# Sums of weight blocks for the last two groups: made on GpSimd alone, their stores asked for later, and one raw quarter stored as it is rounded

## The chip, the core and the metric

The kernel runs on one core of a Trainium2 chip. The metric is the device time of one execution in microseconds (us), as the median of several runs. All of it is in fp32.

## What is computed

Attention in chunks of 64 tokens on 8 batches, 8 heads, 576 tokens and 64 channels, then a mixing block. Cut to what matters:

```python
out = softmax(q_c @ k_c.T / 8) @ v_c                 # chunk by chunk
x = out.transpose(0, 2, 1, 3).reshape(8, 576, 512)
u = x + real(fft2(x))                                # over tokens and channels
un = (u - mean) / sqrt(var + 1e-6)
return u + maximum(un @ w_ch1, 0) @ w_ch2            # 512 -> 2048 -> 512
```

The two weight products are most of the work. `w_ch1` is 512 x 2048, `w_ch2` 2048 x 512; both arrive in 64 bit and are rounded to fp32 on the chip.

## The kernel before, in words

**Groups and steps.** The 4608 tokens are nine groups of 512 (numbers 0 to 8), each of four tiles of 128 rows. A group goes through an *up* product (to 2048 features, `h1`) and a *down* product (back to 512). The generator `mlp(g)` yields after each small part of that; the loop at L1489 counts these yields as *steps* `t`. After each step it hands out a share of the other work: attention and Fourier transform of the next batch, rounding of weight pieces (`round_next`), sums of weight blocks, and loads and stores. No scheduler moves anything: every engine runs its instructions in the order in which this loop writes them down, and so do the queues of transfers. Nearly all transfers are in SyncE's queue, called SP here; some output stores are in ACT's. In the built program each transfer of these two queues waits for the one eight before it.

**Fewer products.** Group 0 multiplies plainly, group 1 plainly in its up product. The other up products, and the down products of groups 1 to 6, split the matrices in halves and use 7 block products in place of 8 (`up_halves`, `down_halves`). In `up_halves` four *pairs* of feature blocks are made one after the other, each in seven *turns* of eight matmul instructions, in the order `UP`. Of a pair, ACT copies a first result (L1272), VectorE adds the others out of PSUM (L1273, L1275, L1277, L1283, L1286), and ACT applies the relu (L1281, L1284, L1287). After each turn SP fetches a slab of summed weights for ten turns later (`fetch(1)`, L1140). In the last turns of pair 2 of groups 7 and 8, GpSimd makes six sums of activation blocks (`EARLY`, L1168).

**26 products in the last two groups.** The down products of groups 7 and 8 (`down_few`, from `FEW = NG - 2`) split finer: 26 products (`PRODUCTS`), of which each reads one block of `w_ch2` or a sum of such blocks. Eighteen sums, the names that begin with s, are used by products (`STORED`). `MADE` lists the 23 operations, intermediate ones too:

```python
MADE = (
    "u=b41-b31", "s3=b31-b41", "s15=u-b42", "s7=u-b11", "s8=b12+b22", "s0=u-s8", "t=b32-b42", "s19=u+t",
    "v=b32-b31", "s10=b11-b12", "s23=v-s10", "s21=s10-b32", "s24=s10-b22", "w=b22-b21", "s22=w-s10",
    "s4=b42-b41", "s25=w+s4", "s1=b21-s4", "s17=b21+b41", "h=b12+b32", "s12=h-s17", "s6=b42-h", "s18=-h",
)
```

`make_rest` does this in two halves, since there is little room: for each it loads the eight raw blocks (L1109), each 128 x 512, makes the sums (L1121, the negation at L1117), and stores the eighteen that are used (L1127) to DRAM (`s3`). It has fourteen places of 128 x 512, kept in the list `spare`: a place is given back when its block is last used, and an operation that takes it again must wait until the store out of it has landed. In before, a store is written into SP's queue when the next used sum has been written down (`behind` holds one), and the work goes to GpSimd for every third operation and to VectorE for the others. `make_rest` is advanced by one or two of its yields after each step from step 203 on, that is in the down product of group 6 and the up product of group 7. At step 225, in the last pair of group 7's up product, what is left of it is written down and the first six slabs of group 7's down product are fetched (`fetch(3)`, L1143).

**Raw quarters.** The blocks that the products read unsummed are stored to DRAM too: three quarters of `w_ch2` by `keep2_whole` (L1079), as the pieces are rounded in group 0, and the last by `keep2_last` (L1083), four stores of 256 KB in steps 32 to 35, at the start of group 1. Rounding of a piece ends with L386 on VectorE; L346 loads the next one. In group 1 SP also carries the loads of k (L250), which VectorE transposes (L416) before a head product (L448) can start.

**Outputs.** When a tile's down product is summed, `store` asks for it: L1027 on SP for one half of the tiles, L1036 on SP and ACT for the other. In group 6 the sums before them are L1335 and L1338 on VectorE. In the same product GpSimd makes L1330 and L1331 and VectorE makes the operands of the next group (L994, L1005, L1015 to L1018).

Of the kernel before, what the change touches and what calls it, by code (L numbers as in the profile page):

```python
# [11 lines left out]
ALU = mybir.AluOpType  # L12
# [4 lines left out]
def kernel(  # L17
# [32 lines left out]
    nc = tc.nc  # L50
# [10 lines left out]
    KF = DFF // 128  # L61
# [41 lines left out]
    NO, HF = 7, KF // 2  # L103
# [989 lines left out]
    def make_rest():  # L1093

        z, spare = Z3 // 2, []
        for i in range(4):
            spare.append(xall[:, 2 * G:2 * G + 4, :].rearrange("p a f -> p (a f)")[:, i * z:(i + 1) * z])
        for tag, n in (("q", 2), ("k", 2), ("zf", 2), ("two", 1), ("qT", 1), ("kT", 1), ("pT", 1)):  # L1100
            t = one_p.tile([128, n * z], FP32, tag=tag, name="part")
            spare += [t[:, i * z:(i + 1) * z] for i in range(n)]
        last = {x: i for i, text in enumerate(MADE) for x in text.replace("=", "-").replace("+", "-").split("-")}
        for half in range(2):
            part = slice(half * z, (half + 1) * z)
            where, behind = {}, []
            for name in ("b31", "b41", "b42", "b11", "b12", "b22", "b32", "b21"):
                where[name] = spare.pop(0)
                nc.sync.dma_start(out=where[name], in_=block_of(name)[:, part])  # L1109
                if name in ("b41", "b11", "b22"):  # L1110
                    yield
            for i, text in enumerate(MADE):
                name = text.split("=")[0]
                to = spare.pop(0)
                if "=-" in text:
                    used = [text.split("-")[1]]
                    nc.vector.tensor_scalar(to, where[used[0]], -1.0, None, ALU.mult)  # L1117
                else:
                    name, *used, op = parsed(text)
                    in0, in1 = (where[x] for x in used)  # L1120
                    (nc.gpsimd if i % 3 == 1 else nc.vector).tensor_tensor(out=to, in0=in0, in1=in1, op=op)  # L1121
                where[name] = to
                if name in STORED:
                    behind.append(name)
                while behind and (len(behind) > 1 or i == len(MADE) - 1):
                    old = behind.pop(0)
                    nc.sync.dma_start(out=block_of(old)[:, part], in_=where[old])  # L1127
                spare += [where[x] for x in (*used, name) if last[x] == i]
                if i % 2:
                    yield  # L1130

    FEW = NG - 2
# [281 lines left out]
    with tc.manual_schedule():  # L1414
        nc.vector.memset(warm, 0.0)
        make_identity(nc, ident)
        nc.vector.memset(eps, 1e-6)
        for r in range(4):
            nc.vector.memset(sign[32 * r:32 * r + 32], 2.0 * (r % 2) - 1.0)
        nc.vector.memset(top[:, 0:1], float((896 + 255) << 20))  # L1420
        nc.vector.memset(top[:, 1:2], float(255 << 23))
        nc.scalar.preload_act_table_set("natural_log_exp_and_others")
        first_rest = three_p.tile([128, XW], FP32, tag="y", name="first_rest")
        for t in more_v + v_ring:
            nc.vector.memset(t[:, :, :, D:DV], 1.0)
        for n in range(first[1]):
            load(n)
            if n < 3:
                load_v(n)
        load_v(3)  # L1430
        load_v(4)
        load_tables()
        load_weight(0)
        load_dim_tables()
        for i in range(1, len(spaces)):
            load_weight(i)
        n_w = 2
        idle = [ps_f.tile([128, 512], FP32, tag="ff", name="idle")]
        early_xp = [ps_f.tile([128, 512], FP32, tag="ff", name="early_xp") for _ in range(2)], None

        def keep_warm(times):

            for _ in range(times):
                nc.tensor.matmul(out=idle[0][:, 0:NQ], lhsT=warm[:, 0:128], rhs=warm[:, 0:NQ], start=True, stop=True)

        put_off, first_ups = [], []

        def round_next(later=None):
            nonlocal n_w
            if n_w <= len(pieces):  # L1450
                round_weight(n_w, later)
                n_w += 1

        keep_warm(8)
        attention_early()
        turn_dim_row()
        for step, _ in enumerate(fourier_early()):
            if step == 0:
                turn_dim_tables()
        round_next()  # L1460
        PAUSE = 3

        def side(b):
            yield from attention(b)
            for _ in range(PAUSE if b == 1 else PAUSE - 1):
                yield
            yield from fourier(b)

        sides = [list_ for list_ in (side(b) for b in range(1, B))]
        sizes = []  # L1470
        for b in range(1, B):
            n_tiles = first[b + 1] - first[b]
            sizes.append((4 * n_tiles + 1 if b == 1 else 3 * n_tiles + 1) + PAUSE + 2 + (b == 1) + NM + b % 2)
        done, cur = 0, 0
        begin = [0]
        for g in range(NG):
            begin.append(begin[-1] + (KF if g < first_of[1] else 2 * HF) + (KF if g < first_of[2] else 2 * NO if g < FEW else NR2 // 2))
        ready_at = [begin[g] + (2 * KF - 7 if g < first_of[2] else 2 * HF + 4) for g in range(NG)]
        conv2 = iter([step for i in range(HF // 2) for step in [keep2(i ^ 1)]])
        conv1 = iter([step for i in range(4) for step in [keep1(i)]])  # L1480

        def chain(gens):
            for gen in gens:
                yield from gen

        n_whole, late, rest_ = 0, [], None
        conv2, conv1 = chain(conv2), chain(conv1)
        t = 0
        for g in range(NG):  # L1489
            for _ in mlp(g):  # L1490
                t += 1
                heavy = False
                for do in late:
                    do()
                late = []
                if t == 8:
                    nc.scalar.copy(tk, early_tk[:, :, :, 0:NE])
                if cur < len(sides):
                    t0 = 3 if cur == 0 else ready_at[cur - 1]
                    t1 = ready_at[cur]  # L1500
                    due = min(sizes[cur], (t - t0) * sizes[cur] // (t1 - t0))
                    while done < due:
                        heavy = next(sides[cur], None) or heavy
                        done += 1
                    if t >= t1:
                        for _ in sides[cur]:
                            pass
                        cur, done = cur + 1, 0
                if not heavy:
                    round_next(late if t < KF and t % 4 == 3 else None)  # L1510
                    if t <= 2 or t < KF and t % 4 == 0 or t >= KF + 3:
                        round_next()

                while n_whole < HF // 2 and n_w > KF + HF + 2 * n_whole + 2:
                    keep2_whole(n_whole)
                    n_whole += 1
                if n_w > len(pieces):
                    for _ in range(3):
                        next(conv2, None)
                if t == begin[1] - 1:  # L1520
                    for _ in conv2:
                        pass
                if begin[1] <= t < begin[1] + HF // 2:
                    keep2_last(t - begin[1])
                if t > ready_at[FEW - 1]:
                    rest_ = rest_ or make_rest()
                    for _ in range(1 + t % 2):
                        next(rest_, None)
                if t == begin[FEW] + 2 * HF - 3:
                    for _ in rest_:  # L1530
                        pass
                    for _ in range(NS3):
                        fetch(3)
                if begin[1] <= t < begin[1] + KF // 2:
                    for _ in range(3):
                        next(conv1, None)
                if t == begin[1] + KF // 2:
                    for _ in range(NS2):
                        fetch(2)
                if t == begin[1] + KF:  # L1540
                    for _ in range(NS1):
                        fetch(1)
# [49 lines left out]
```

## Time and profile before

| what | value |
|---|---|
| median of 4 runs | 1097.84 us (1094.62 to 1098.67) |
| the profiled execution | 1097.19 us, span 1095.4 us |
| busy share of TensorE, VectorE, ACT, GpSimd | 97%, 55%, 28%, 35% |
| mean granted TensorE clock | 0.99 |
| transfers | 219.53 MB, mean 200 GB/s |
| group 6 down (827.0 to 881.5 us) | 54.5 us, TensorE busy 53.31 |
| group 7 up (881.5 to 949.7 us) | 68.2 us, TensorE busy 56.57 |
| group 8 up (996.4 to 1044.7 us) | 48.3 us, TensorE busy 48.30 |

A row of a window gives its bounds, its length, the busy time of TensorE, of its weight load, of VectorE, ACT and GpSimd (in brackets the instructions), the granted clock, the share of the transfer engines and GB/s. A row of the timeline gives start, duration, engine, line, operation, tiles and shapes, and in square brackets how long the engine was idle before it and on whom. A row of waits gives who waited for whom: us in total, times, and the longest. A piece of the chain gives its start, its length and what it is; a transfer's length there is from its issue to its landing. PE is TensorE, DVE is VectorE, POOL is GpSimd, SPq is SyncE's queue. PE's busy time includes its modelled pipeline, so a slow clock shows as longer matmuls.

### The profile page before, as it was taken

The page shows a single profiled execution, that of the slowest core. Times are in us where ns is not written, and L with a number is a line of the kernel's source. Part 1 is how long each engine was busy: PE and PEld are TensorE (multiplying, and loading weights), DVE is VectorE, ACT ScalarE, POOL GpSimd, SP SyncE. Part 2 cuts the span into 40 slices and gives each one's busy share as a digit, 9 for nine tenths or more (in the row PEclk, how much of TensorE's full clock was granted, in tenths as well). Part 3 has the DMA queues.
Part 4 walks back from the last instruction along what each step waited for, and adds up shares of the span by engine and source line. Part 5 has one row for each costly group of instructions (what it writes and reads, how often), then busy time and mean ns, then how long its engine had stood idle before and what let it go on. Part 6 is the DMA issues. An engine that isn't in the chain of part 4 may idle for free.

```text
span 1095.4 us, 19948 instructions
## 1 busy us (share of the span) xinstructions
PE 1059.3 (97%) x7386; PEld 839.2 (77%) x7386; DVE 603.7 (55%) x1305; ACT 310.7 (28%) x728; POOL 387.9 (35%) x509
## 2 busy tenths in 40 slices
PE   8999989999999999999999999999999987999997
PEld 6645444446888888888888888888888866888886
DVE  4798975233567455654565556645655636334331
ACT  4687653212113411322033203330223001201200
POOL 4311017463515140345033401632243414470281
PEclk9999999999999999999999999999999988999999
DMA  8677566598467645873677357935643668887366
GB/s 175 212 208 210 130 183 210 179 313 273 150 190 225 162 165 163 243 212 127 190 208 220 123 160 238 246 114 176 231 135 129 218 208 294 313 303 247 110 220 202
DMA packets 162829, 219.53 MB, mean 200 GB/s; under 512 B 69644, under 2 KB 107532, under 8 KB 157358
## 3 DMA queue, kind: packets, MB, share of 16 engines
q1 hardware_dynamic: 159084, 214.86, 63.5%
q10 hardware_dynamic: 3330, 2.76, 1.0%
q8 instruction: 59, 0.97, 0.4%
q0 software_dynamic: 320, 0.66, 0.3%
q14 instruction: 36, 0.29, 0.1%
HBM read 183.61 MB, written 34.60 MB: 199 GB/s over the span
## 4 chain that ended last, share of the span: by engine, by line
PE 74%; DMA 7%; DVE 6%; POOL 3%; ACT 3%; SPq 3%; issue 3%; ACTq 0%; DVEq 0%; POOLq 0%
PE pa L1267 17%; PE pb L1318 14%; PE pb L1267 12%; PE pa L1318 11%; PE dn L1382 8%; PE up L1200 2%; PE pt L397 2%; DMA s<-part 2%; PE up L1180 2%; PE mix L838 2%; SPq L263 1%; PE z L719 1%; PE xp L498 1%; DMA xall<-in_moe_w_ch_dram 1%; PE sc L448 1%
## 5 line engine op out<-in xcount | busy, mean ns | idle before, releaser
L1267 PE MATMUL pa<-unT,wa 128*128 128x256 f32 x672 | 163.8, 387 | 11.0 <-DVE wa L1275 4.9
L1267 PEld LDWEIGHTS pa<-unT,wa 128*128 128x128 f32 x672 | 127.8, 193 | 31.0 <-DVE wa L1275 6.1
L1267 PE MATMUL pb<-wa 128*128 128x256 f32 x448 | 107.7, 383 | 1.6 <-DVE h L1286 1.6
L1267 PEld LDWEIGHTS pb<-wa 128*128 128x128 f32 x448 | 85.1, 192 | 13.9 <-DVE h L1286 2.0
L1318 PE MATMUL pa<-wb,h 128*128 128x256 f32 x384 | 87.2, 380 | 0.0
L1318 PE MATMUL pb<-wb,h 128*128 128x256 f32 x384 | 86.4, 379 | 0.0
L1318 PEld LDWEIGHTS pa<-wb,h 128*128 128x128 f32 x384 | 71.8, 190 | 9.7
L1318 PEld LDWEIGHTS pb<-wb,h 128*128 128x128 f32 x384 | 72.0, 190 | 9.4
L1154 POOL TENSOR_TENSOR h<-h 128x256 f32<-128x256 f32 x48 | 40.8, 858 | 94.3 <-DVE wb L1152 91.1
L555 POOL COPY xall<-xall 1x512 f32<-1x512 f32 x28 | 17.9, 639 | 147.9 <-DVE xall L515 120.4
L1382 PE MATMUL dn<-wb,h 128*128 128x256 f32 x304 | 67.6, 379 | 0.0
L1382 PEld LDWEIGHTS dn<-wb,h 128*128 128x128 f32 x304 | 57.4, 190 | 7.6
L1273 DVE TENSOR_TENSOR wa<-pb,wa 128x256 f32<-128x256 f32 x56 | 23.7, 424 | 63.9 <-ACT wa L1272 63.9
L1221 PE MATMUL dn<-wb,h 128*128 128x512 f32 x128 | 58.7, 607 | 0.0
L1200 PE MATMUL up<-unT,wa 128*128 128x512 f32 x128 | 58.5, 610 | 0.0
L1168 POOL TENSOR_TENSOR h<-h 128x512 f32<-128x512 f32 x36 | 45.5, 1279 | 33.5 <-ACT h L1287 30.2
L1272 ACT COPY wa<-pa 128x256 f32<-128x256 f32 x56 | 20.9, 373 | 125.4 <-PE pa L1267 94.7
L1267 PE MATMUL pa<-wa 128*128 128x256 f32 x224 | 55.7, 393 | 0.1
L1267 PE MATMUL pb<-unT,wa 128*128 128x256 f32 x224 | 53.2, 380 | 0.0
L1281 ACT ACTIVATE h<-pa 128x256 f32<-128x256 f32 x56 | 21.6, 385 | 106.3 <-PE pa L1267 105.6
L1180 PE MATMUL up<-unT,wa 128*128 128x512 f32 x108 | 49.4, 598 | 0.0
L1267 PEld LDWEIGHTS pa<-wa 128*128 128x128 f32 x224 | 42.9, 195 | 7.3 <-ACT wa L1272 0.8
(290 smaller groups left out, 1993.5 us busy)
## 6 DMA issues: line engine op xcount, KB each, us to landing
wa<-s SPq DMA_DIRECT2D x196, 256.0 KB
wb<-s SPq DMA_DIRECT2D x42, 1024.0 KB
wb<-s SPq DMA_DIRECT2D x52, 512.0 KB
xall<-in_moe_w_ch_dram SPq DMA_DIRECT2D x22, 512.0 KB
q<-in_q_dram SPq DMA_DIRECT2D x96, 112.0 KB
k<-in_k_dram SPq DMA_DIRECT2D x96, 112.0 KB
v<-in_v_dram SPq DMA_DIRECT2D x124, 64.0 KB
s<-part SPq DMA_DIRECT2D x27, 256.0 KB
```

The lines of the kernel that those rows point to most:

```text
L397: nc.tensor.transpose(pt[:, j, :], src(j), ident)
L838: nc.tensor.matmul(out=mix[:, cols], lhsT=zt[:, T], rhs=tab, start=(T == 0), stop=(T == 3), skip_group_check=True,)
L1154: nc.gpsimd.tensor_tensor(out=h1[:, m, hi], in0=h1[:, m, lo], in1=h1[:, m, hi], op=ALU.subtract)
L1168: nc.gpsimd.tensor_tensor(out=out_, in0=a, in1=b, op=op)
L1180: nc.tensor.matmul(out=up, lhsT=w1[:, kk, m * 128:(m + 1) * 128], rhs=unT[:, kk], start=(kk == 0), stop=(kk == KD - 1), skip_group_check=True,
L1200: nc.tensor.matmul(out=up, lhsT=w1[:, kk, m * 128:(m + 1) * 128], rhs=unT[:, kk], start=(kk == 0), stop=(kk == KD - 1),)
L1221: nc.tensor.matmul(out=dn, lhsT=h1[:, m, s * 128:(s + 1) * 128], rhs=w2[:, m, :], start=(m == 0), stop=(m == KF - 1),)
L1267: nc.tensor.matmul(out=dst, lhsT=w[:, kk, r], rhs=rhs[o][:, kk], start=(o in (0, 1) and kk == 0), stop=(kk == 1), skip_group_check=True,)
L1273: nc.vector.tensor_tensor(out=b, in0=pbs[r][:, 0], in1=a, op=ALU.add)
L1281: nc.scalar.activation(out=h1[:, m, lo], in_=dst, func=ACTF.Relu)
L1318: nc.tensor.matmul(out=dst, lhsT=lhs[:, m], rhs=w[:, m], start=(o in (0, 2) and m == 0), stop=(m == HF - 1), skip_group_check=True,)
L1382: nc.tensor.matmul(out=dst, lhsT=lhs[:, m], rhs=w[:, m], start=(fresh and not half and m == 0), stop=(m == 3), skip_group_check=True,)
```

## The change

```diff
@@ make_rest
             for name in ("b31", "b41", "b42", "b11", "b12", "b22", "b32", "b21"):
                 where[name] = spare.pop(0)
                 nc.sync.dma_start(out=where[name], in_=block_of(name)[:, part])
-                if name in ("b41", "b11", "b22"):
+                if half and name in ("b41", "b11", "b22"):
                     yield
+            yield
             for i, text in enumerate(MADE):
                 name = text.split("=")[0]
                 to = spare.pop(0)
                 if "=-" in text:
                     used = [text.split("-")[1]]
-                    nc.vector.tensor_scalar(to, where[used[0]], -1.0, None, ALU.mult)
+                    nc.scalar.mul(to, where[used[0]], -1.0)
                 else:
                     name, *used, op = parsed(text)
                     in0, in1 = (where[x] for x in used)
-                    (nc.gpsimd if i % 3 == 1 else nc.vector).tensor_tensor(out=to, in0=in0, in1=in1, op=op)
+                    nc.gpsimd.tensor_tensor(out=to, in0=in0, in1=in1, op=op)
                 where[name] = to
                 if name in STORED:
                     behind.append(name)
-                while behind and (len(behind) > 1 or i == len(MADE) - 1):
+                done_with = [x for x in (*used, name) if last[x] == i]
+                while behind and (len(behind) > 3 or i == len(MADE) - 1):
                     old = behind.pop(0)
                     nc.sync.dma_start(out=block_of(old)[:, part], in_=where[old])
-                spare += [where[x] for x in (*used, name) if last[x] == i]
+                    if last[old] <= i and old not in done_with:
+                        done_with.append(old)
+                spare += [where[x] for x in done_with if x not in behind]
                 if i % 2:
                     yield
@@ the loop over steps
-                if begin[1] <= t < begin[1] + HF // 2:
-                    keep2_last(t - begin[1])
-                if t > ready_at[FEW - 1]:
-                    rest_ = rest_ or make_rest()
+                while n_last < HF // 2 and n_w > KF + 2 * n_last + 2:
+                    keep2_last(n_last)
+                    n_last += 1
+                if t == ready_at[FEW - 1]:
+                    rest_ = make_rest()
+                    next(rest_)
+                if t > ready_at[FEW - 1] + 4:
                     for _ in range(1 + t % 2):
                         next(rest_, None)
```

- All 44 two-operand sums of `make_rest` go to GpSimd (before: 14, and 30 on VectorE); the two negations go from VectorE to ACT.
- The eight loads of the first half are written down together at step 202 instead of over the first steps from 203; the sums follow from step 207 on instead of right after the loads. The loads of the second half still come in parts, at steps 214 to 216; its sums run to step 224.
- A store is written down when three further used sums have been (`behind` holds three), and a place is not given back before its store has been asked for.
- The four stores of `keep2_last` are written down as soon as the two pieces that they read are rounded, in group 0, among SP's weight loads, instead of in steps 32 to 35.
- TensorE's instructions and their order are the same.

More of the change, by code (lines that the diff above doesn't have):

```diff
@@ L1484, in chain @@
                 yield from gen
-        n_whole, late, rest_ = 0, [], None
+        n_whole, n_last, late, rest_ = 0, 0, [], None
         conv2, conv1 = chain(conv2), chain(conv1)
```

## The prediction

> **What bounds the kernel now.** I read the page's engine shares first, then busy time by windows around the two stages that the diff touches, then TensorE's waits there, the timeline and the chain of waits.
>
> ```profile
> PE 1059.3 (97%) x7386; PEld 839.2 (77%) x7386; DVE 603.7 (55%) x1305; ACT 310.7 (28%) x728; POOL 387.9 (35%) x509
> ...
> 881.50:949.70 68.20, 56.57 (x227) 46.64 (x226) 32.26 (x60) 13.64 (x31) 20.21 (x15) 0.90 0.79 262
> ...
> 996.40:1044.70 48.30, 48.30 (x225) 42.53 (x224) 16.98 (x40) 13.93 (x31) 8.01 (x7) 1.00 0.40 132
> ```
>
> TensorE sets the time, so only its gaps and its slow clock can be won. The two windows are the up products of group 7 and of group 8: the same matmuls take 68.2 us and 48.3 us, so group 7 loses 19.9 us (11.6 idle, the rest at a granted clock of 0.90). Its waits say on whom:
>
> ```profile
> PE pa L1267 <- DVE wa L1275: 3.8, 2, 2.0
> PE pa L1267 <- DVE h L1283: 3.3, 1, 3.3
> PE pa L1267 <- DVE wb L1338: 2.9, 1, 2.9
> PE pb L1267 <- DVE h L1286: 1.6, 1, 1.6
> ```
>
> All four are VectorE evictions standing behind a weight sum (L1121) that waits for a transfer:
>
> ```profile
> 883.64 0.69 DVE L1121 TENSOR_TENSOR part<-part,xall 128x512 f32<-128x512 f32 x1 [4.73 <-DMA s<-part]
> ...
> 889.44 3.78 PE L1267 MATMUL pa<-wa 128*128 128x256 f32 x8
> ...
> 907.18 3.66 PE L1267 MATMUL pa<-unT,wa 128*128 128x256 f32 x8 [3.28 <-DVE h L1283]
> ```
>
> Eight matmul instructions take 1.73 us elsewhere: after 3 us of idling the next eight cost 1.9 to 2.1 us more.
>
> The other place is group 1, where two head products wait for a k load:
>
> ```profile
> 212.56 0.69 PE L448 MATMUL sc<-kT,qT 64*64 64x64 f32 x32 [1.45 <-DVE rd L511]
> ...
> 230.15 0.69 PE L448 MATMUL sc<-kT,qT 64*64 64x64 f32 x32 [1.89 <-DVE rd L511]
> 230.77 4.11 PE L1200 MATMUL up<-unT,wa 128*128 128x512 f32 x5
> ```
>
> **Part 1, raw quarter earlier.** Four stores of 256 KB (L1083) leave SP's queue at 201.24, 209.21, 216.45 and 219.05 us. There SP asks without pause and the transfers run at 370 GB/s (window 210 to 215 us), 0.71 us for each. The k load of 203.78 has one of them ahead: 0.7 us off the 1.45. The k load of 224.20 has all four ahead, 2.8 us, and TensorE arrives 0.7 earlier: the 1.89 goes. Then the clock need not fall: 5 instructions took 4.11 us where 16 take 7.13 (2.2 for five), 1.9 us. Sum 4.5 us, with nothing below 0 in it since the queue only loses work. Up to 262 us no other wait of TensorE shows, and from 262 to 770 only 1.0 us, so it is kept.
> The same stores now stand among the weight loads of 105 to 134 us, each asked behind the eviction L386 of its second piece. Most is covered: VectorE waits there 1.4 us in all for a load, and v, q and k have slack. One store stands just ahead of the loads of 136.44 and 139.09, where VectorE already waits 0.51 and 0.85 us, and TensorE later 2.1 us. Cost between 0 and 1.4 us (two stores wholly exposed); I take one, 0.7. Net 3.8 us won.
>
> **Part 2, sums on GpSimd.** VectorE loses 30 sums of 0.69 us and 2 negations (0.42 and 1.48), 22.6 us, so its evictions follow TensorE at once; they read PSUM, and none of L1273 to L1286 is over 0.426 us anywhere, also beside GpSimd. Four two-SBUF additions beside it, L1015 to L1018, do stretch (0.415 to 1.381 us), as they did before. GpSimd now has 44 sums, and ACT the negations. What is late next is that chain, and it ends in ACT's queue: the second negation (s18 = -h) stands between the last relu of pair 2 and L1272 of pair 3, and turn 2 of pair 3 waits for L1272. So every later step of the stage waits for GpSimd's sum h. I walk to it on the clock of before:
>
> ```profile
> 875.11 9.15 DMA s<-part
> ...
> 904.03 6.73 DMA s<-part
> ...
> 963.00 8.94 POOL L1168 TENSOR_TENSOR h<-h 128x512 f32<-128x512 f32 x7
> ```
>
> - First half: all eight blocks are asked for one step earlier and at once (from 843.5 us) and land by 857; GpSimd is free at 857.9 (end of L1331). Ten sums at 1.28 (8.94 / 7) end near 871. The eleventh, s23, overwrites s7, whose store is asked for behind the output stores L1027, at about 872.4 (873.38 before, less one sum and its wait). A store in that place took 9.15 us: s23 starts at 882.6.
> - Twelve sums to s6: 12 x 1.28, 897.9. SP stands at that store with the second half's loads behind it. ACT's first negation is done at 896 while the relu L1281 behind it was due at 889, so turn 6 of pair 0, which waits for that relu, stalls by about 5 us; that adds nothing to the end, which the second negation sets. While SP stands at a store, slabs stand behind it: each is asked for ten turns (17.3 us) ahead, SP is 10 us late at worst, so this is hidden; with another 7 us it would be paid in full.
> - From 898.5 SP asks for 8 loads and 7 slabs, then the store of the new s3, each transfer waiting for the one eight before it. Before, 14 such left between 895.28 and 904.03, 0.63 us each: s3 is asked at 908, lands 5 us later (eight places of 0.63; the row of 904.03 gives 6.73): 913.2.
> - The sum t overwrites s3. From it to h are 14 weight sums and, in between, 5 sums of the activations (L1168): 19 x 1.28, 937.5.
> - Negation 0.63 (as L1287), L1272 0.37, turns 2 to 6 of pair 3 5 x 1.73, slow clock after 11 us idle 2.0: the stage ends at 949.1. Before, the first down product started at 949.54. The six first slabs are asked for near 941.6, behind the last stores (941.48 before), and GpSimd's last activation sum ends near 941.4: neither is late for the down product.
>
> Part 2 is worth 0.4 us: 20 us of stalls are removed and 20 come back behind GpSimd. Ends: with 6.73 for the landing, 1.7 us later; with sums of 1.59 (the longest L1168 on h), 6 us later; if the pair of output stores holds s7 for 6.73 and not 9.15, 2.4 earlier; if no transfer holds GpSimd in the second half, its 20 sums to h and the 5 others follow 897.9 directly and end at 929.9, 7.6 earlier. So from 8 won to 8 lost; I take the walk's value, whose rows come from the same places in the queue.
>
> **A rule.** Row: a sum is 0.69 us on VectorE and 1.28 on GpSimd, 1.85 times. The Trainium skill, GPSIMD Engine Reference, section 4.1 Engine selection, speaks against the change: elementwise work belongs on VectorE, GpSimd being about twice slower with two inputs. By its factor, an estimate, a sum is 1.38 and the 19 end 2 us later, near 1095.5 us in all.
>
> **Sum.** The profiled execution took 1097.19 us (span 1095.4). Less 3.8 and 0.4: 1093.0; the median of the runs shown is 0.65 above that execution, so 1093.6.
>
> **Rivals.**
> - *Slower: GpSimd as the bound.* Each us that h is late is a us of the stage. It decides once h is later than 941.7 (part 1 eaten up) and is over the measurable from 945. For it: the 3 sums of 1.5 us and more beside VectorE in before; SP's stores, slabs and loads in one queue. Sums at 1.59 and a landing of 6.73 give 8 us: 1093.6 + 8 = 1101.5. Against: in the up stage VectorE has no two-SBUF work left. 0.23.
> - *Much faster: the chain is not last.* If the output stores do not hold s7, the first half ends 10 us sooner and the second half's first loads land near 894: 25 sums later h is done at 926 and the stage at 937.6, 11.5 us more: 1082. For it: GpSimd idles 11 us before s23 in my walk. Against: the 9.15 us row. 0.15.
> - *Part 1 gives nothing* (the k load held by something else in the queue): 1097.4. 0.17. That the change doesn't do what it says is excluded: the built order shows 44 sums on GpSimd, none on VectorE.
> - Forecast, 1089 to 1096: 0.45.
>
> **How the numbers follow.** About 0.3%, 3.3 us, can be told from no change: under 1094.5 faster, over 1101.1 slower. Of the forecast's 0.45 some 0.32 lies under 1094.5; with the fast rival's 0.15 that is faster 0.47. Its other 0.13 and the third rival's 0.17 are same, 0.30. Slower is the first rival, 0.23. The range of 8 in 10 leaves out about half of each outer rival: 1085 to 1102.
>
> **What would show it.** Right: 44 sums at 1.27 on GpSimd; no DVE L1121 kind in the stage; the wait of pair 3's turn 2 for ACT, about 11 us near 926 to 938, and a shorter one in pair 0; the sum s23 waiting 10 us for a store; both k waits near 212 and 230 us gone or below 1 us. Wrong: pair 3 not waiting for ACT (then h was early), a stage of group 7 under 60 us or over 72, or new waits of TensorE between 140 and 165 us above 5 us in all (the moved stores cost more).

## The result

| | median (runs) | ratio to the kernel before, 95% interval |
|---|---|---|
| before | 1096.06 us (73) | |
| changed | 1098.05 us (44) | 1.0020 (1.0012 to 1.0028) |

The change costs 2.0 us where 4.2 were forecast to be won (1093.6 against 1097.84). That is inside the 0.3% that the prediction calls no change, and inside the range given, but on the other side, and the interval leaves out no change. The profiled execution took 1098.73 us, span 1096.8 us, 1.4 more than that of before.

The page's engine shares, the rows of time by windows for the up products of group 7 and group 8, and TensorE's waits between 870 and 965 us. (Lines behind the edited function are four higher than in before: L1267 is L1271, L1121 is L1122, L1127 is L1129, L1140 is L1144.)

```profile
PE 1054.0 (96%) x7386; PEld 836.4 (76%) x7386; DVE 583.5 (53%) x1273; ACT 311.4 (28%) x730; POOL 422.1 (38%) x539
```

```profile
878.90:950.40 71.50, 52.83 (x227) 44.87 (x226) 16.81 (x40) 14.35 (x33) 50.05 (x41) 0.88 0.75 260
997.70:1046.00 48.30, 48.30 (x226) 42.51 (x224) 16.99 (x40) 13.76 (x31) 7.85 (x7) 1.00 0.41 133
```

```profile
PE pa L1271 <- ACT wa L1276: 14.9, 2, 14.2
PE pa L1271 <- ACT h L1285: 3.8, 1, 3.8
...
PE dn L1386 <- DMA wb<-s: 0.4, 1, 0.4
```

VectorE has lost half of its work in the stage (32.3 to 16.8 us, third busy column) and no wait names it there any more. In its place two waits name ACT, and the stage is 3.4 us longer (71.3 us, from 878.99 to 950.32; before 67.9, from 881.66 to 949.54). ACT's timeline says why it is late:

```profile
893.33 0.63 ACT L1118 ACTIVATE xall<-part 128x512 f32<-128x512 f32 x1 [9.75 <-POOL part L1122]
893.87 0.64 ACT L1285 ACTIVATE h<-pa 128x256 f32<-128x256 f32 x2
...
938.82 0.63 ACT L1118 ACTIVATE part<-part 128x512 f32<-128x512 f32 x1 [15.69 <-POOL part L1122]
939.36 0.63 ACT L1276 COPY wa<-pa 128x256 f32<-128x256 f32 x2
```

These are the two negations of h. Each stands until GpSimd has made h, and the relu or the copy that TensorE needs is the next instruction of ACT. GpSimd's timeline shows where that chain itself stood:

```profile
867.55 1.45 POOL L1122 TENSOR_TENSOR part<-xall,part 128x512 f32<-128x512 f32 x1
880.37 1.27 POOL L1122 TENSOR_TENSOR part<-part 128x512 f32<-128x512 f32 x1 [11.36 <-DMA s<-part]
...
894.60 1.27 POOL L1122 TENSOR_TENSOR part<-xall,part 128x512 f32<-128x512 f32 x1
905.19 2.49 POOL L1122 TENSOR_TENSOR part<-part 128x512 f32<-128x512 f32 x2 [9.32 <-DMA part<-s]
...
914.87 1.27 POOL L1122 TENSOR_TENSOR part<-part,xall 128x512 f32<-128x512 f32 x1 [2.14 <-DMA s<-part]
```

Three stops of over a microsecond from s23 on: 11.4 us for the store of s7, 9.3 us for the raw blocks of the second half, 2.1 us for the store of s3. Part 1 shows in the head products of group 1, in TensorE's timeline:

```profile
211.55 0.69 PE L448 MATMUL sc<-kT,qT 64*64 64x64 f32 x32 [0.25 <-DVE rd L511]
...
227.74 0.70 PE L448 MATMUL sc<-kT,qT 64*64 64x64 f32 x32 [0.51 <-DVE rd L511]
228.37 7.13 PE L1204 MATMUL up<-unT,wa 128*128 128x512 f32 x16
```

The waits of 1.45 and 1.89 us are down to 0.25 and 0.51, and the clock no longer falls behind them: the sixteen instructions of the last row take 7.13 us, where before they took 8.83 at a granted clock of 0.80. At 235 us TensorE is 4.1 us ahead of before, when group 7 begins 2.7; at the first down product of group 7 it is 0.8 behind, at the end 1.4.

### The profile page after: what moved, and what is told of

Same layout as the page of the kernel before. It is cut to its first block, busy times and chain, and to the rows that moved or that the text cites. A ratio compares the mean times of both kernels' runs of the same rounds, so it can differ in the third digit from the quotient of the medians.

```text
span 1096.8 us, 19948 instructions
## 1 busy us (share of the span) xinstructions
PE 1054.0 (96%) x7386; PEld 836.4 (76%) x7386; DVE 583.5 (53%) x1273; ACT 311.4 (28%) x730; POOL 422.1 (38%) x539
## 4 chain that ended last, share of the span: by engine, by line
PE 70%; DMA 9%; DVE 5%; POOL 5%; SPq 3%; issue 3%; ACT 3%; DVEq 0%; POOLq 0%; ACTq 0%
PE pa L1271 15%; PE pb L1322 14%; PE pa L1322 11%; PE pb L1271 11%; PE dn L1386 8%; DMA s<-part 3%; DMA wb<-s 3%; PE up L1204 2%; PE pt L397 2%; POOL part L1122 2%; SPq L263 2%; PE mix L838 2%; PE z L719 1%; PE xp L498 1%; PE up L1184 1%
## 5 line engine op out<-in xcount | busy, mean ns | idle before, releaser
L1271 PE MATMUL pa<-unT,wa 128*128 128x256 f32 x672 | 160.5, 382 | 7.1 <-ACT h L1285 3.8
L1271 PEld LDWEIGHTS pa<-unT,wa 128*128 128x128 f32 x672 | 126.3, 190 | 25.3 <-ACT h L1285 4.2
L1271 PE MATMUL pb<-wa 128*128 128x256 f32 x448 | 107.8, 384 | 0.0
L1271 PEld LDWEIGHTS pb<-wa 128*128 128x128 f32 x448 | 85.3, 192 | 12.1
L1271 PE MATMUL pa<-wa 128*128 128x256 f32 x224 | 55.8, 393 | 14.9 <-ACT wa L1276 14.9
L1271 PEld LDWEIGHTS pa<-wa 128*128 128x128 f32 x224 | 42.7, 195 | 22.2 <-ACT wa L1276 15.7
L1271 PE MATMUL pb<-unT,wa 128*128 128x256 f32 x224 | 53.0, 379 | 0.0
```

The source lines that it names most:

```text
L1271: nc.tensor.matmul(out=dst, lhsT=w[:, kk, r], rhs=rhs[o][:, kk], start=(o in (0, 1) and kk == 0), stop=(kk == 1), skip_group_check=True,)
```

## The experiments

Theory after the result: the mechanism was as worked out (the chain on GpSimd ends in ACT's queue), but the chain's second half starts later than worked out, because of what stands ahead of its loads in the queue of transfers. Rivals: part 1 does not pay; ACT's queue alone is at fault; GpSimd's rate alone is.

**The two parts, each by itself.** `e1_part1` is the kernel before with the early raw quarter; `e2_part2` is the changed kernel without it.

```diff
 e1, on before                                        e2, on the changed kernel
-if begin[1] <= t < begin[1] + HF // 2:              -while n_last < HF // 2 and n_w > KF + 2 * n_last + 2:
-    keep2_last(t - begin[1])                        -    keep2_last(n_last)
+while n_last < HF // 2 and n_w > KF + 2*n_last + 2: -    n_last += 1
+    keep2_last(n_last)                              +if begin[1] <= t < begin[1] + HF // 2:
+    n_last += 1                                     +    keep2_last(t - begin[1])
```

> The kernel before with one thing of the change alone: the four stores of the raw quarter asked for as their pieces are rounded; the weight sums stay as they were. Theory: in the trace of the changed kernel TensorE is 4.1 us ahead of the kernel before at 235 us, and 2.7 us ahead when group 7 begins, since 1.4 us are given back at 450 and 679 us, where a load of q sets VectorE's next step and follows only in part. So this kernel is 2.7 us faster than the one before (ratio 0.9975), with the waits of 1.45 and 1.89 us near 212 and 230 us down to 0.5 or less. Rival 1: what is given back at 450 us is chance of one profile, then 4 us faster (0.9963). Rival 2: what is won in group 1 is lost again later, within 0.5 us of the kernel before.

> The changed kernel with the raw quarter's stores back in steps 32 to 35: the weight sums part alone. Theory: the changed kernel is 2.0 us slower than the one before although its first part wins 2.7, so this part alone costs 4.7 us (ratio 1.0043), and TensorE waits for ACT before the last pair of group 7 as in the changed kernel (14 us). Rival: the first part is worth nothing by the end, because the chain on GpSimd ends at a time that does not hang on TensorE's pace; then this kernel takes as long as the changed one, 2.0 us over before (1.0018).

Measured: e1 0.9977 (0.9960 to 0.9995), 2.5 us faster, e2 1.0039 (1.0020 to 1.0058), 4.3 us slower. They add to what both did together (+1.8 against +2.0 us): within these intervals the parts are independent, part 1 pays, and part 2 is a loss. In e1's timeline TensorE is 3.5 us ahead at 235 us and gives some of it back at two places where VectorE stands for a load of q:

```profile
450.31 1.99 PE L1267 MATMUL pa<-unT,wa 128*128 128x256 f32 x8 [1.61 <-DVE wa L1275]
...
677.86 1.99 PE L1267 MATMUL pa<-unT,wa 128*128 128x256 f32 x8 [1.56 <-DVE wa L1275]
```

Before, these waits were 0.55 and 0.50. But e2, without part 1, has 1.93 and 1.72 there, so whether part 1 pushes into them or the one profile of before was lucky stays open.

**ACT's queue alone?** `e3_neg_pool` takes the negations out of ACT.

```diff
-nc.scalar.mul(to, where[used[0]], -1.0)
+nc.gpsimd.tensor_scalar(to, where[used[0]], -1.0, None, ALU.mult)
```

> The changed kernel with the two negations on GpSimd in place of ACT: ACT no longer waits for the sums, so the 14 us wait of TensorE for ACT before the last pair of group 7, and the one of 3.8 us in the first pair, must go. Theory: this moves the wait and does not remove it. GpSimd has two operations more (2.5 us), the last sums end near 944 us, the six first slabs of the down product stand behind their stores in SP's queue and land from about 951 us; the up stage ends near 932 us, TensorE then waits 15 to 19 us for a slab, and the total is 0 to 3 us over that of the changed kernel (1.002 to 1.005 of before). Rival: only ACT's queue holds TensorE; then the down product begins near 932 us and the total is 15 us or more under the changed kernel (0.988).

Measured: 1.0058 (1.0040 to 1.0076), some 4 us over the changed kernel, a little more than expected. Both long waits for ACT are gone. TensorE's timeline at the start of the down product:

```profile
950.26 5.60 PE L1386 MATMUL dn<-wb,h 128*128 128x256 f32 x16 [18.57 <-DMA wb<-s]
```

The down product starts at 950.26 in place of 950.32. The wait was not removed, it moved to the slab that stands behind the chain's last stores: a visible wait taken away, with the chain behind it unchanged, gains nothing.

**The first half alone.** `e4_ahead` writes the first half's sums, and so their stores, ahead of group 6's outputs (step 208), and leaves everything else where it was.

```diff
-for _ in range(1 + t % 2):
+ahead = {ready_at[FEW - 1] + 6 + i: 9 if i == 0 else 0 for i in range(6)}
+for _ in range(ahead.get(t, 1 + t % 2)):
```

> The changed kernel with the first half's sums (up to s6) all written down by step 208, before the output stores of group 6, so that their stores stand ahead of those outputs in SP's queue; the negation, the four last stores and the second half stay where they were. Theory: the chain of GpSimd was held 11.4 us by the store of s7, which stood behind an output pair. That wait goes, the first half ends near 885 us and not at 896, the second half's loads are asked for some 9 us earlier (SP still stands until the last outputs, 886 us), the sum h is done near 930 in place of 938.75, TensorE's wait before the last pair shrinks to 4 to 6 us, and the total falls by 8 to 11 us from the changed kernel's (0.992 to 0.995 of before). Rival: the second half's start is set by the queue of transfers behind the outputs and slabs anyway; then h moves by under 3 us and the total by under 3 us.

Measured: 1.0036 (1.0018 to 1.0054). My theory fell, the rival held. GpSimd's timeline, then SP's queue, then one piece of the chain that ended last, of this run:

```profile
885.27 1.27 POOL L1122 TENSOR_TENSOR part<-xall,part 128x512 f32<-128x512 f32 x1
906.22 2.49 POOL L1122 TENSOR_TENSOR part<-part 128x512 f32<-128x512 f32 x2 [19.69 <-issue]
```

```profile
884.82 1.16 SPq L1027 DMA_DIRECT2D out_dram<-wb  x2
...
899.52 1.48 SPq L1109 DMA_DIRECT2D part<-s  x2
```

```profile
885.39 11.61 DMA out_dram<-wb
```

The stop for s7 is gone and the first half is done 9 us sooner. The second half starts at 906.2 all the same (905.2 before this edit): its loads are asked for at 899.5, behind output stores of which the last landed 11.6 us after it was asked for. So s7, which the prediction timed to 0.4 us, was not what set the end.

**Why those outputs are slow, and what they hold.** A store of L1027 is 128 KB with its rows in reverse. When nothing else is under way the window row is

```profile
1001.00:1003.90 2.90, 2.90 (x15) 2.55 (x14) 1.55 (x4) 0.37 (x1) 0.00 (x0) 1.00 0.13 35
```

The transfer engines are 13% busy, as much as two of sixteen, at 35 GB/s, where the window from 897 to 914 us of the same kernel reaches 352. The Trainium skill, DMA: Bandwidth & Descriptors, section on why a DMA increments its semaphore by 16, says that a transfer uses the largest number of engines up to 16 that divides the slowest dimension of both sides; here that dimension is 2 (a 2 x 32 x 512 pattern), so rule and row agree. `e9_no_low` leaves these four stores of group 6 out:

```diff
+if n in groups[6]:
+    continue
 nc.sync.dma_start(out=to, in_=o[r0:r0 + CH])          # L1027
```

> The changed kernel with the four stores of line 1027 of group 6 left out (these rows of the output are not stored); nothing is moved. Theory: those four stores, which use two of sixteen transfer engines, are what delays both halves of the sums, the first through the store of s7 and the second through the loads behind them. Then the wait of 11.4 us for s7's store shrinks to 2 or less, the second half's first sum starts near 893 to 896 and not 905.2, the sum h is done near 927 to 930 in place of 938.75, TensorE's 14 us wait before the last pair falls to 4 us or less, and the total is 9 to 12 us under the changed kernel (0.991 to 0.994 of before). Rival: the second half waits for the queue as a whole (15 transfers of 256 KB and the stores before them); first sum at 902 or later and a total within 3 us of the changed kernel.

Measured: 0.9969 (0.9947 to 0.9990), some 5.5 us under the changed kernel. The second half's first sum and TensorE's last pair, two rows of its timelines (lines two higher):

```profile
896.21 2.50 POOL L1124 TENSOR_TENSOR part<-part 128x512 f32<-128x512 f32 x2 [11.57 <-DMA part<-s]
```

```profile
930.95 3.78 PE L1273 MATMUL pa<-wa 128*128 128x256 f32 x8 [12.28 <-ACT wa L1278]
```

The second half starts 9.0 us sooner and the last pair 8.8 us sooner than in the changed kernel. The total moved by less than the 9 to 12 us expected, and the wait for ACT is still 12 us long, because TensorE, no longer held in pair 0, arrives sooner too. So the outputs hold the chain, and with them gone it is still last.

**Undoing the engine.** `e12_split` gives 30 of the sums back to VectorE and keeps the rest of the change.

```diff
-nc.gpsimd.tensor_tensor(out=to, in0=in0, in1=in1, op=op)
+(nc.gpsimd if i % 3 == 1 else nc.vector).tensor_tensor(out=to, in0=in0, in1=in1, op=op)
```

> The changed kernel with the two-operand sums back on both engines as before (every third on GpSimd, the rest on VectorE); early loads, later stores, negations on ACT and the raw quarter as changed. Theory: the chain is shorter (h near 920) and TensorE no longer waits for ACT before the last pair, but VectorE stands at sums that wait, first for GpSimd behind s7's store (to 883 us), then for the second half's loads (to 905 us), and its evictions behind them: the stage loses some 12 to 18 us as in the kernel before, total between 4 us under and 1 us over before (0.996 to 1.001). Rival: with the stores later VectorE need not stand any more; the stage loses under 8 us, the total is 8 us or more under before (0.993).

Measured: 0.9966 (0.9950 to 0.9982), some 6 us under the changed kernel (1.0020), inside the range that its theory gave. TensorE waits for VectorE again, as in before, and hardly for ACT; its waits between 876 and 945 us, and the longest in the timeline:

```profile
PE pa L1271 <- DVE wa L1279: 6.0, 3, 2.7
PE pa L1271 <- ACT wa L1276: 1.6, 1, 1.6
```

```profile
925.37 3.68 PE L1271 MATMUL pa<-unT,wa 128*128 128x256 f32 x8 [2.71 <-DVE wa L1279]
```

The down product begins at 944.63, 5.7 us sooner. Of the whole change the engine is the part that costs: the same queue, loads and stores with two engines make the end earlier by more than the stalls that this brings back. Beside e1 (0.9977) the other edits to the sums (early loads, later stores) show no loss, and no gain that these intervals can tell.

**Moving the outputs to another queue.** In `e5_out_act` (on the changed kernel), `e6_before_out_act` (on before) and `e8_burst_out_act` (on e7 below) ACT asks for L1027.

```diff
-nc.sync.dma_start(out=to, in_=o[r0:r0 + CH])
+nc.scalar.dma_start(out=to, in_=o[r0:r0 + CH])
```

> The changed kernel with the output stores of line 1027 (128 KB each) asked for on ACT's queue in place of SP's. New theory: these stores are what holds the chain of sums, twice over. In the kernel where the first half was written down ahead of them, the last landed 11.6 us after it was asked for, and two of them land 2.5 to 2.7 us apart where a slab of 256 KB takes 0.63; while only they are under way (1001 to 1003.9 us of the changed kernel) the transfer engines are 12% busy, two of sixteen. The Trainium skill (DMA: Bandwidth & Descriptors, section on why a DMA increments its semaphore by 16) says that a transfer is spread over the largest number up to 16 that divides the slowest dimension of both sides, and that dimension is 2 here. In SP's queue everything behind them waits for those two engines; from ACT's queue they run beside SP's transfers. Then the store of s7 is asked for near 860 us and not 871, the 11.4 us wait goes, and the second half's loads no longer queue behind two pairs: first sum of the second half near 895 to 898 in place of 905.2, the sum h 7 to 10 us earlier, and the waits of 2.2 and 1.1 us at 450 and 679 us shrink. Total 8 to 11 us under the changed kernel (0.991 to 0.995 of before). Rival: the sixteen transfer engines are one pool whatever the queue; s7 moves but the second half's loads land as late as before, and the total moves by under 3 us.

> The kernel before with the same move alone: the stores of line 1027 on ACT's queue. Theory: the waits of VectorE's sums for stores that stand behind those outputs (4.7 us before 883.64 us, and the later ones) shrink, so that the up products of group 7 lose 8 to 14 us in place of 19.9; with the k load near 212 us no longer behind four such stores the 1.45 us wait goes as well. Total 5 to 11 us under before (0.990 to 0.995). Rival: nothing but the asking moves; within 2 us of before, or slower by up to 3 where ACT now stands at a store that waits for VectorE.

Measured: e5 1.0095 (1.0073 to 1.0117), e6 1.0036 (1.0020 to 1.0052). Both worse, which I had left to a rival for e6 and not seen at all for e5. TensorE's waits in e5:

```profile
PE pa L1271 <- ACT wa L1276: 22.9, 5, 16.8
```

ACT stands at each output until VectorE has summed it (it asks at 883.82 after a sum that ended at 883.78, and in an earlier group at 307.01 after one that ended at 306.98), and the copies that TensorE needs stand behind. The second half's first sum came at 915.7, with TensorE 11.0 us behind the changed kernel when group 7 begins: the loads had gained nothing from the other queue.

**Writing all sums early.** `e7_burst` takes e3's negations and writes the first half by step 208 and the second right behind it.

```diff
-for _ in range(1 + t % 2):
+for _ in range(9 if t == ready_at[FEW - 1] + 6 else 1 + t % 2):
```

> The changed kernel with the whole of the weight sums written down as early as they can be: first half by step 208 (ahead of the outputs of group 6), the second half right behind it from step 209, and the two negations on GpSimd, so that neither ACT nor TensorE stands behind the chain. Theory: GpSimd runs 23 operations of 1.27 us from 854.7 us with one wait of 2.6 us, done near 886; the second half's loads stand behind the first output pair only, its sums start near 892 and end near 925 to 928, the six slabs land from 934 us, and the down product of group 7 begins near 935 in place of 950.3: 13 to 17 us under the changed kernel (0.987 to 0.990 of before). Rival: the outputs hold the second half's loads as in the run that wrote only the first half ahead (first sum at 906); then the down product begins near 945 and the gain is 5 us at most.

> Both together: the sums written down early, negations on GpSimd, and the stores of line 1027 on ACT's queue. Theory: with nothing of the outputs in the way, the second half's sums start near 888 to 890 and end near 920; the up product of group 7 takes 48 to 50 us and ends near 928, the slabs land by 930, and the total is 20 to 24 us under the changed kernel (0.980 to 0.984 of before), the fastest of all. Rival: one pool of transfer engines; as the run without the move, within 3 us of it.

Measured: e7 0.9943 (0.9922 to 0.9964), 6 us under before and 8 under the changed kernel; e8 1.0020 (1.0006 to 1.0035). e8 was to be the fastest and is 8 us over e7: TensorE waits 17.2 us for ACT there, as in e5. e7 beats both kernels, by half of what was expected. Its down product begins at 942.82. ACT's timeline shows a stop that I had not counted:

```profile
875.96 17.09 ACTq L1036 DMA_DIRECT2D out_dram<-wb  x4
893.15 0.65 ACT L1276 COPY wa<-pa 128x256 f32<-128x256 f32 x2 [29.71 <-DMA xall<-s]
```

ACT asks for half of the L1036 outputs (10.0 us for the four in the changed kernel). Each must wait for the transfer eight before it, and those are now the chain's, behind L1027: VectorE's last sum there ends at 881.3, and the third of the four is asked for at 891.5. The copy behind waits too, and TensorE 9.3 us with it. `e10_burst_sp` (on e7) gives ACT's share of group 6's L1036 to SP; `e11_burst_pool` besides has GpSimd ask for L1027 there, in a queue of its own.

```diff
-eng = nc.scalar if r else nc.sync                          # L1036, e10 and e11
+eng = nc.scalar if r and n not in groups[6] else nc.sync
-nc.sync.dma_start(out=to, in_=o[r0:r0 + CH])               # L1027, e11 alone
+(nc.gpsimd if n in groups[6] else nc.sync).dma_start(out=to, in_=o[r0:r0 + CH])
```

> The kernel with the sums written down early, with the second halves of group 6's output stores (line 1036) on SP like the first, so that ACT asks for no transfer there. That kernel had a new wait of 9.3 us in the first pair of group 7: ACT stood at such a store, which waits for the transfer eight before it, and the copy L1276 stood behind. Theory: the wait goes, but the first slab of the down product lands at 941 to 942 as before, since GpSimd's chain is not touched; TensorE waits there instead, and the total moves by under 2.5 us. Rival: ACT is what sets the end now; then 7 to 9 us less (0.986 to 0.988 of before).

> The same, with group 6's four stores of line 1027 asked for by GpSimd, in a queue of its own, right behind the first half's sums (they are done by then, so GpSimd does not stand). Theory: SP's loads and stores of the second half no longer queue behind them; the waits of 7.8 us for loads and 6.1 us for the store of s3 fall to 2 or 3 us each, the sums are done near 922, the slabs land from 930 us, the down product begins near 931 to 934, and the total is 8 to 11 us under the run with line 1036 on SP (0.983 to 0.987 of before). Rival: the two transfer engines are shared whatever the queue, and GpSimd pays for the asking; within 3 us of that run.

Measured: e10 0.9964 (0.9944 to 0.9985), e11 0.9971 (0.9951 to 0.9991). For e10 the theory held in the total, within 2.5 us of e7, and in that ACT is no longer waited for; but the wait came back at a slab in pair 1 (7.1 us), not at the down product. For e11 the rival held. A piece of its chain, a load of the second half in SP's queue while the four outputs were under way in GpSimd's:

```profile
892.43 9.38 DMA part<-s
```

It took 9.4 us to land; in e10, with the outputs in SP's own queue, the longest load on the chain took 8.3 us, and in the changed kernel 6.0. The second half's first sum came at 900.6, 4.1 us later than in e10: a queue of their own for the outputs does not free the others here. The stores are not quite the same there, since GpSimd's queue moved them in 1075 packets of some 0.5 KB (886 to 900 us), so what the queue alone would do stays open.

**Which of the two holds the early version: outputs or rate?** `e13_defer` (on e10) asks for the four L1027 stores in steps 215 and 218; `e14_shared` (on e10) gives ten of the second half's last fifteen operations to VectorE, from step 218; `e15_both` does both.

```diff
+if t in (ready_at[FEW - 1] + 13, ready_at[FEW - 1] + 16):   # e13: two of the stores held back
+    for _ in range(2):
+        to, from_ = held.pop(0)
+        nc.sync.dma_start(out=to, in_=from_)
-nc.gpsimd.tensor_tensor(out=to, in0=in0, in1=in1, op=op)     # e14
+shared = half and i >= 8 and i % 3 != 1
+(nc.vector if shared else nc.gpsimd).tensor_tensor(out=to, in0=in0, in1=in1, op=op)
```

> The early sums with group 6's outputs on SP only, and the four stores of line 1027 put off: two are asked for in step 215 and two in step 218, behind slabs of group 7. Theory: it is the place of these four stores, ahead of the second half's loads, that costs. The first sum of the second half starts near 891 to 893 (896.5 without), the wait of 6.6 us for the store of s3 falls to 2.5 or less, and so does the 7.4 us wait of TensorE for a slab; the down product of group 7 begins 8 to 11 us sooner, and the total falls by as much (0.987 to 0.990 of before). Rival: the two transfer engines are the bound over the whole stage, so that the stores cost the same wherever they stand; within 3 us of the run without (0.994 to 0.998).

> The early sums with outputs on SP only, and of the second half's fifteen last operations ten on VectorE, written down from step 218 on, when what they read has landed. Theory: GpSimd's rate is what delays the last sums; with 10 operations of 0.69 us beside 5 of 1.27 they end near 922 and not 932, the first slab of the down product lands near 934, and TensorE waits for it 1 to 3 us after an up product that ends near 931 to 935 (its slab waits of 7 us stay): 5 to 9 us less (0.988 to 0.992 of before). Rival: SP stands at transfers, not at sums; the first slab lands at 940 or later and the total stays within 2 us (0.995 to 0.998).

> Both: the four stores of line 1027 put off and the second half shared with VectorE. Theory: the up product of group 7 runs in 49 to 52 us, the slabs are there when it ends, the down product begins near 930 to 933: 11 to 14 us under the run with neither (0.984 to 0.987 of before). Rival: as for the two alone, within 3 us of it.

Measured: e13 0.9960 (0.9937 to 0.9984), e14 0.9945 (0.9929 to 0.9961), e15 0.9990 (0.9968 to 1.0011). None reached what was expected. In e13 the second half's first sum came at 892.1 as expected, but slabs were late instead (4.2 and 3.6 us of waits); in e15 VectorE stood 12.6 us at a shared sum behind GpSimd, itself waiting for a store (10.4 us of TensorE). In e14 a slab in pair 1 was 7.9 us late, and the sums ended at 930, not 922. The line's view of that run (least, median and longest ns) shows one reason:

```profile
L1123 DVE TENSOR_TENSOR part<-xall,part x4: 678/1552/1748, 919.5 to 923.7; 128x512 f32<-128x512 f32 x4
```

A sum that takes VectorE 0.68 us alone took up to 1.75 us while GpSimd summed beside it. The other reason is again a store: GpSimd stood 4.0 us for one at 918 us. The down product began at 940.2 in e13, 943.2 in e14 and 945.1 in e15, against 944.6 in e10 (the profiled execution of e13 is its fastest, 2.1 us under its median). Moving one item in the queue of transfers made another late each time. What would have to be shortened is the sum of the transfers there, and no run did that.

## Why the prediction was wrong, and where it was right

Part 1 was right. 4.5 us were forecast up to 235 us, less 0.7 for the moved stores; the trace shows 4.1 in the changed kernel and 3.5 in e1, and both k waits have all but gone, as described. "So it is kept" did not hold: of the 4.1 us only 2.7 are left when group 7 begins, and most of the rest goes at 450 us. By the end it is worth 2.5 us (0.5 to 4.4), an interval that holds the forecast of 3.8.

Taken as a time, the forecast (1093.6 against 1098.05) is 4.5 us off; taken as a change (4.2 won, 2.0 lost) it is 6.2 off. That the time looks better is chance: the four runs from which it started lie 1.8 us over the median of 73.

Part 2 was forecast at 0.4 won and measured 4.3 lost (2.2 to 6.4). The mechanism was right at each joint: s23 waits 11.4 us for s7's store (forecast 10), ACT's first negation holds pair 0 for 3.8 us (5), the second holds pair 3 for 14.2 us (11), no VectorE wait is left in the stage. The walk's times, less the 2.7 us by which the stage began sooner, stand against the trace so:

| step of the walk | walk | trace |
|---|---|---|
| s23 starts | 879.9 | 880.37 |
| first half's sums end | 895.2 | 895.87 |
| SP asks for the second half's first load | 895.8 | 897.85 |
| SP asks for the store of s3 | 905.3 | 909.34 |
| it has landed | 910.5 | 914.80 |
| h is done | 934.8 | 938.8 |
| first down product | 946.4 | 950.32 |

The step that failed is one: "From 898.5 SP asks for 8 loads and 7 slabs, then the store of the new s3 ... 0.63 us each". SP's queue in the changed kernel:

```profile
897.85 1.35 SPq L1109 DMA_DIRECT2D part<-s  x2
899.31 0.88 SPq L1144 DMA_DIRECT2D wa<-s  x2
900.24 0.42 SPq L1109 DMA_DIRECT2D xall<-s  x1
901.25 2.22 SPq L1109 DMA_DIRECT2D part<-s  x3
903.56 0.59 SPq L1144 DMA_DIRECT2D wa<-s  x1
905.08 0.32 SPq L1109 DMA_DIRECT2D part<-s  x1
905.73 0.32 SPq L1109 DMA_DIRECT2D xall<-s  x1
906.43 2.25 SPq L1144 DMA_DIRECT2D wa<-s  x4
909.34 0.32 SPq L1129 DMA_DIRECT2D s<-part  x1
```

```profile
897.00:914.00 17.00, 17.00 (x76) 14.74 (x75) 4.99 (x13) 4.78 (x11) 7.45 (x6) 0.94 1.00 352
```

The count, 15 transfers, was right. The price was not: 11.5 us, 0.77 each, where 0.63 had been taken from fourteen asks of before. That was the spacing of asks, not of transfers. The window row of before for the same asks:

```profile
895.00:904.00 9.00, 7.34 (x33) 5.81 (x31) 2.97 (x6) 1.92 (x4) 1.76 (x1) 1.00 0.86 279
```

At 279 GB/s fewer than ten blocks of 256 KB move in these 9 us, while fourteen were asked for: SP ran ahead of the transfers. In the row of the changed kernel the transfer engines are 100% busy at 352 GB/s, 256 KB at that rate are 0.74 us, and SP asks no faster than that. With the outputs left out (e9) the same fifteen asks, from 888.78 to 900.01, still took 0.75 us each, so this price is not the outputs'. And the first load was 2.0 us late, since the walk let SP ask for it 0.6 us after the last sum was done, while the last stores of the first half (asked for at 896.16 and 896.69) stood ahead. Together that is 4.0 us, and it runs through to the down product (3.9). The other misses are small: part 1 gives 1.1 us less at that point, and after the stage another 0.6 us are lost, most of it a slab that is 0.45 us late. The three make the 5.6 us by which the span (1096.8) is over the one forecast (1095.4 less 4.2).

How far the outputs stand behind this was not seen either. The prediction took a landing of 9.15 us as a price "in that place" without asking why; e9 shows that the four L1027 stores cost the chain 9 us, and e4 that they cost it even when s7 is out of their way. With that known, the fast rival (the outputs don't hold s7, 1082) could have been struck out: in e4 they no longer hold s7, and it was no faster, since the loads of the second half stand behind the same stores. Only with the outputs left out (e9) does the second half start near the rival's time, at 896.2, and the total falls by 5.5 us. The slower rival, GpSimd as the bound, came nearest: its deciding point was h at 941.7 on the clock of before, and h came at 941.5; but not by its price, since the sums took 1.27 us and not 1.59. The rule that was weighed, that VectorE and not GpSimd is the place for such sums (the Trainium skill, GPSIMD Engine Reference, section 4.1), pointed the right way: a sum took the 1.27 us of the row, but e12 shows that 6 us hang on the choice of the engine.

## What to carry to other kernels

When work is moved off an engine that stalls, follow the last value of the moved chain to the queue that waits for it, then price everything that must go through the transfer engines before that value: number of transfers times bytes over the rate of a full window, not the spacing of a few asks. A wait that a profile names is only the last one to end: taking it away (e3, e4, e10) moved the loss to the next queue each time, and only more engines for the chain, an earlier start of it or less in the queue moved the end. Where a landing is many times longer than the transfer's bytes need, find out what stands ahead and why, before using it as a price.

## What was not expected of the hardware

- A 128 KB store with a 2 x 32 x 512 pattern keeps the transfer engines 13% busy at 35 GB/s; asking for four of them from GpSimd's queue (e11) did not free SP's transfers, of which a load asked for beside them took 9.4 us to land (8.3 in e10, with the outputs in SP's queue).
- VectorE's sums of two SBUF blocks stretched from 0.68 to 1.55 us (median of four) and 1.75 us (longest) beside GpSimd's in e14; sharing a chain between the two is worth less than their separate durations say.
- An engine that asks for a transfer can be held by transfers of another engine's making: ACT stood 17.1 us at four L1036 outputs (e7), some 10 of them after VectorE's last sum, with the copy that TensorE needed behind them.
